# Turning the score matrices by DMA at both ends of a window-attention backward kernel, with its first loads and weight products in another order

## The chip, the cores and the metric

The kernel runs on one core of a Trainium2 chip. The metric is the device time of one execution in microseconds (us); of several runs the median is taken. A core has five engines that are used here: TensorE (PE; its weight loads are shown as a row of their own, PEld), VectorE (DVE), ScalarE (ACT), GpSimd (POOL) and SyncE (SP, which only issues DMAs). Each works through its own instructions in order and waits for the others by semaphores. ACT and POOL issue DMAs from their queues too.

## What is computed

The forward pass is windowed attention without heads: an image of 256 x 256 positions and 384 channels is cut into 8 x 8 windows of 64 tokens, 1024 of them. The kernel returns the output and the gradients of x, wqkv and wo for a given gradient of the output, all in bfloat16.

```python
qkv = xw @ wqkv                       # xw: (1024, 64, 384)
q, k, v = qkv[..., :C], qkv[..., C:2 * C], qkv[..., 2 * C:]
p = softmax(einsum('bqc,bkc->bqk', q, k) * C ** -0.5, axis=-1)
o = einsum('bqk,bkc->bqc', p, v) @ wo
# reference: (o, *vjp of o with respect to x, wqkv, wo, applied to grad_out)
```

## The kernel before

**Weights are multiplied with each other first.** With A = scale * Wq Wk^T and B = Wv Wo (both 384 x 384), the scores of a window are x A x^T, its output is P (x B), and the backward pass needs only A, B and their transposes AT and BT. So the kernel begins with turning weight blocks on PE (`turn_blocks`, L94) and multiplying them (`weight_product`, L101): BT and A first; B and AT come in `weight_rest` (L112), which runs inside the first full step.

**Tiles.** 128 partitions hold two windows. Four such pairs make a quad (8 windows, 512 tokens); there are 128 quads, numbered i. For each quad the kernel holds xq and dq (tokens of x and of the gradient on partitions), xT and dT (the same turned, channels on partitions), yz (the projections of dT by BT and of xT by A, channels on partitions), zy (yz in another order, written by VectorE in `gather`), tok (zy turned back to tokens by DMA), ps (P and dS, bfloat16) and PS (P and dS turned). Loads are in `load` (L123: x by SP, the gradient by POOL; in the loop, half of x by ACT in `load_rest`, L131). xT and dT are made by transposing DMAs from SP's queue (`load_turn`, L135), except for the first quads, whose numbers are below X_ON_PE = 1 and G_ON_PE = 4: these are turned on PE (`turn_on_pe`, L143).

**The loop is pipelined by hand.** `step(c, b, a, ahead)` (L346) writes out the order for three quads at once, c = i - 1, b = i, a = i + 1, and starts the loads of quad i + 3. In the order of PE:

- scores of b (`scores`, L180: the tile sd, both x A x^T and the gradient of P), after which VectorE and ScalarE run the softmax and its backward in six pieces (`soft`, L192);
- eight products x B and x AT of b (`uv`, L227: uq and vq), each emptied by ScalarE (L235);
- three products dT BT of a, emptied by ScalarE into yz (L165), then three products xT A (L167); between them in the program stand the end of the softmax and `turn` (L237);
- one row of a finished group's weight gradient (`gf_rows`, L308, tile pg), if there is one;
- the attention of c in four parts (`attend`, L254): pw, pu, po and pd, emptied as Wq (ACT), Uq (DVE), o (ACT) and d (both), with halves of a weight-gradient row (`gf_halves`, L316, tile ph) between them.

`turn` on VectorE turns P and dS in 32 x 32 blocks: one instruction over the whole tile (L240), four for the crossed blocks (L244). PSUM has a ring of eight banks for all products, so a product waits until the bank that it reuses has been emptied.

**Groups.** Every GQ = 3 quads make a group, whose weight-gradient rows (six, from Uq and Wq) fill the later steps; up to and including the step that scores quad 3 there is nothing to fill with. At the end, rows that are left over run after the loop (L474), then the last group's six rows (`gf_final`, L330) and the products that make the weight gradients (`weight_gradients`, L399), stored by SP and ACT.

**The order at the start** (L437 to L452): weights by SP and ACT, nine warm-up products, loads of quads 0, 1 and 2, the turn and product for BT, the turns of quad 0 (dq, then xq), the turns and product for A, the clearing of GF_acc on VectorE. The loop begins at i = -1, a step with only an `a`, which projects quad 0; after the steps i = -1, 0 and 1 the dq of quads 1, 2 and 3 are turned on PE (L462).

Of the kernel before, what the change touches and what calls it, by code (L numbers as in the profile page):

```python
# [9 lines left out]
ALU = mybir.AluOpType  # L10
# [13 lines left out]
def kernel(  # L24
# [47 lines left out]
    def columns(k):  # L72
        return slice(k * C, (k + 1) * C)

    def fetch_weights():
        nc.sync.dma_start(out=w_sb[:, :, columns(2)], in_=w_in[:, :, columns(2)])
        nc.scalar.dma_start(out=wo_sb[:], in_=wo.rearrange("(m p) n -> p m n", p=P))
        for k in (0, 1):
            nc.scalar.dma_start(out=w_sb[:, :, columns(k)], in_=w_in[:, :, columns(k)])

    def warm_up(n):
        zero = B_sb[:].rearrange("p m c -> p (m c)")[:, 0:4 * P]
# [27 lines left out]
                copy_out(mr, dst[:, mr, :], pc[:])  # L110

    def weight_rest():  # L112
        weight_product(B_sb, wT[2], wo_sb, None)
        weight_product(AT_sb, wT[1], wT[0], scale)

    def windows(ap, st, first, count=2):
        row, col = st["at"]
        return ap[0, row + WIN * first:row + WIN * (first + count), col:col + WIN, :]

    LO, HI = slice(0, WT), slice(WT, P)  # L120
    OTHER = {0: HI, WT: LO}

    def load(st, on_act=0):  # L123
        st["xq"] = xq = grp.tile([P, QUAD, C], BF16, tag="xq", name="xq", bufs=2 * GQ + 4)
        st["dq"] = dq = qp.tile([P, QUAD, C], BF16, tag="dq", name="dq", bufs=6)
        for t in range(QUAD):
            if t < QUAD - on_act:
                nc.sync.dma_start(out=xq[:, t, :], in_=windows(x, st, 2 * t))
            nc.gpsimd.dma_start(out=dq[:, t, :], in_=windows(grad_out, st, 2 * t))  # L129

    def load_rest(st, on_act):  # L131
        for t in range(QUAD - on_act, QUAD):
# [56 lines left out]
    def over_k(ap, n=P):  # L189
        return ap.unsqueeze(2).broadcast_to([n, QUAD, WT])  # L190

    def soft(st, step):  # L192
        sd = st["sd"]
        if step == 0:
            st["mx"] = mx = sm.tile([P, QUAD], F32, tag="mx", name="mx")
            for w, h in ((0, HI), (1, LO)):
                nc.vector.tensor_reduce(out=mx[h, :], in_=sd[h, :, w, :], axis=AX.X, op=ALU.max)
        elif step == 1:
            mx = st["mx"]
            st["sh"] = sh = sm.tile([P, QUAD, WT], F32, tag="sh", name="sh")  # L200
            for w, h, o in ((0, HI, LO), (1, LO, HI)):
                nc.vector.tensor_tensor(out=sh[o, :, :], in0=sd[h, :, w, :], in1=over_k(mx[h, :], WT),
                                        op=ALU.subtract)
        elif step == 2:
            st["ex"] = ex = sm.tile([P, QUAD, WT], F32, tag="ex", name="ex")
            nc.scalar.activation(out=ex[:], in_=st["sh"][:], func=ACT.Exp)
        elif step == 3:
            ex = st["ex"]
            rs = sm.tile([P, QUAD], F32, tag="rs")
            nc.vector.tensor_reduce(out=rs[:], in_=ex[:], axis=AX.X, op=ALU.add)  # L210
            ri = sm.tile([P, QUAD], F32, tag="ri")
            nc.vector.reciprocal(out=ri[:], in_=rs[:])
            st["ps"] = ps = qp.tile([P, 2, QUAD, WT], BF16, tag="ps", name="ps")
            st["Pb"], st["dS"] = ps[:, 0, :, :], ps[:, 1, :, :]
            nc.vector.tensor_tensor(out=st["Pb"], in0=ex[:], in1=over_k(ri[:]), op=ALU.mult)
        elif step == 4:
            st["pr"] = pr = sm.tile([P, QUAD, WT], F32, tag="pr", name="pr")
            for w, h in ((0, LO), (1, HI)):
                nc.vector.tensor_tensor(out=pr[h, :, :], in0=sd[h, :, w, :], in1=st["Pb"][h, :, :], op=ALU.mult)  # L219
            st["D"] = D = sm.tile([P, QUAD], F32, tag="D", name="D")  # L220
            nc.vector.tensor_reduce(out=D[:], in_=pr[:], axis=AX.X, op=ALU.add)
        else:
            pd = sm.tile([P, QUAD, WT], F32, tag="pd")
            nc.vector.tensor_tensor(out=pd[:], in0=st["Pb"], in1=over_k(st["D"][:]), op=ALU.mult)
            nc.vector.tensor_tensor(out=st["dS"], in0=st["pr"][:], in1=pd[:], op=ALU.subtract)

    def uv(st, t, part):  # L227
# [9 lines left out]
    def turn(st):  # L237
        ps = st["ps"]
        st["PS"] = dst = qp.tile([P, 2, QUAD, WT], BF16, tag="PS", name="PS")
        nc.vector.transpose(out=dst[:].rearrange("p s t k -> p (s t k)"), in_=ps[:].rearrange("p s t k -> p (s t k)"))  # L240
        for first in range(0, P, WT):
            for q in (0, SQ):
                k = SQ - q
                nc.vector.transpose(out=dst[first + k:first + k + SQ, :, :, q:q + SQ].rearrange("p s t k -> p (s t) k"),  # L244
                                    in_=ps[first + q:first + q + SQ, :, :, k:k + SQ].rearrange("p s t k -> p (s t) k"))

    def operand(st, n, t, h):
        if n in ("PT", "ST"):
            return st["PS"][h, int(n == "ST"), t, :]
        if n in ("z", "y"):  # L250
            return st["tok"][h, int(n == "y"), :, t, :]
        return st[n][h, t, :]
# [93 lines left out]
    def step(c, b, a, ahead):  # L346


        def on(st):
            return (lambda f, *r: f(st, *r)) if st is not None else (lambda f, *r: None)  # L350
        C_, B, A = on(c), on(b), on(a)
        B(scores)
        B(soft, 0)
        if b is not None and c is None:
            weight_rest()
        B(uv, 0, 0)
        B(uv, 0, 1)
        B(soft, 1)
        B(uv, 1, 0)
        B(uv, 1, 1)  # L360
        B(soft, 2)
        B(soft, 3)
        B(uv, 2, 0)
        B(uv, 2, 1)
        B(uv, 3, 0)
        B(uv, 3, 1)
        B(soft, 4)
        for mo in range(CK):
            A(project, 0, mo)
        B(soft, 5)  # L370
        B(turn)
        if ahead is not None:
            load(ahead, ON_ACT)
        A(gather, 0)
        for mo in range(CK):
            A(project, 1, mo)
        if ahead is not None:
            load_rest(ahead, ON_ACT)
        if fill:
            gf_rows(*fill.pop(0))  # L380
        slots = attention(c) if c is not None else iter(())
        for t in range(QUAD):
            if t == 2:
                A(gather, 1)
            next(slots, None)
        for rest in slots:
            pass

    G_ON_PE, X_ON_PE = 4, 1
    ON_ACT = 2  # L390
    EV = {"z": "AAA", "y": "AAA", "u": "AAAA", "v": "AAAA", "o": "AAAA", "U": "DDDD", "W": "AAAA", "d": "DADAA"}
    quads = [(row, col) for col in range(0, W, WIN) for row in range(0, H, 2 * WIN * QUAD)]
    sts = [{"at": q, "i": i} for i, q in enumerate(quads)]
    n = len(sts)
    AHEAD = 3
    dw_out = out_2.rearrange("(m p) j -> p m j", p=P)
    dwo_out = out_3.rearrange("(m p) n -> p m n", p=P)
# [1 line left out]
    def weight_gradients(group):  # L399
# [31 lines left out]
        dw = rows("dw")  # L431
        for k in range(CK):
            product_row(k, dw[:, k, :], GFT[1], woT_sb, None)
            (nc.scalar, nc.sync)[k % 2].dma_start(out=dw_out[:, k, columns(2)], in_=dw[:, k, :])

    with tc.manual_schedule(engines=MANUAL):
        fetch_weights()  # L437
        warm_up(9)
        load(sts[0])
        make_identity(nc, ident[:])  # L440
        load(sts[1])
        load(sts[2])
        load_turn(sts[0])
        load_turn(sts[1])
        turn_blocks(wT[2], w_sb, 2 * CK)
        weight_product(BT_sb, wo_sb, wT[2], None)
        turn_on_pe(sts[0], "dq", "dT")
        turn_on_pe(sts[0], "xq", "xT")
        turn_blocks(wT[0], w_sb, 0)
        turn_blocks(wT[1], w_sb, CK)  # L450
        weight_product(A_sb, wT[0], wT[1], scale)
        nc.vector.memset(GF_acc[:], 0.0)  # L452
        held = []
        last = None
        get = lambda i: sts[i] if 0 <= i < n else None
        for i in range(-1, n + 1):
            if 0 <= i < n - 2:
                load_turn(sts[i + 2])
            if 0 <= i < n:
                to_tokens(sts[i])  # L460
            step(get(i - 1), get(i), get(i + 1), get(i + AHEAD) if i >= 0 else None)
            if 0 < i + 2 < G_ON_PE:  # L462
                turn_on_pe(sts[i + 2], "dq", "dT")
            if i == 1:
                turn_blocks(woT_sb, wo_sb)
            if i > 0:
                held.append(sts[i - 1])
                sts[i - 1] = None
            if held and i == n:
                last = gf_final(held)  # L470
            elif len(held) == GQ:
                fill.extend((held, f, ma) for f in range(2) for ma in range(CK))
                held = []
        while fill:  # L474
            gf_rows(*fill.pop(0))
        weight_gradients(last)


# [28 lines left out]
```

## Time and profile before

| | us |
|---|---|
| median of 3 runs | 1917.22 |
| lowest and highest | 1910.97, 1922.25 |
| the profiled execution | 1913.78 |
| its span, first to last instruction | 1912.0 |
| PE busy | 1897.3 (99%) |
| VectorE busy | 1676.1 (88%) |
| ScalarE busy | 1530.4 (80%) |
| POOL busy | 860.0 (45%) |
| mean granted clock of PE | 0.997 |

Times in the profile count from the start of the span. Busy time of PE counts a product from its start to its modelled end, so overlapping products fill it; a group like "PE L151 MATMUL pj<-xT,A_sb" is named by engine, line, operation, output and input. In brackets behind an instruction stands how long its engine idled before it and who ended that. SPq, ACTq and POOLq are the DMA-issuing parts of these engines; the time from a DMA's issue to its landing is listed apart. Marks in the profiled execution: the first scores at 18.25, those of quad 1 at 30.45, of quad 2 at 46.72, of quad 3 at 59.87 and of quad 4 at 74.69; the last quad's scores at 1868.72; the last rows of the last group from 1893.5; the last copy out of PSUM begins at 1908.38.

### The profile page before, as it was taken

The numbers are of one execution on the slowest core, as the hardware profiler recorded it, in microseconds if no ns is written. First come the engines' busy times: TensorE is split into PE (matmuls) and PEld (weight loads), VectorE is DVE, ScalarE is ACT, GpSimd is POOL, SyncE is SP. The second block draws the span as 40 slices with busy tenths as digits, with TensorE's granted clock in tenths as the row PEclk, the third lists the DMA queues.
The fourth block names the chain that finished last, engine by engine and source line by source line (L and its number), as shares of the span: only waits on it lengthen the run. The fifth ranks groups of instructions, "written<-read, shape, count | busy, mean of one in ns | idle before, by whom it ended". The sixth has DMA issues, their size and how long they took to land.

```text
span 1912.0 us, 57287 instructions
## 1 busy us (share of the span) xinstructions
PE 1897.3 (99%) x22359; PEld 1131.5 (59%) x22359; DVE 1676.1 (88%) x3625; ACT 1530.4 (80%) x3357; POOL 860.0 (45%) x1574
## 2 busy tenths in 40 slices
PE   8999999999999999999999999999999999999998
PEld 5556655655665565556556655655665565556555
DVE  6888888888888888888888888888888888888887
ACT  7878887888788888878887887888788788878884
POOL 3444544444444444444444444444444444445432
PEclk9999999999999999999999999999999999999999
DMA  8999999999999999999999999999999999999993
GB/s 183 200 223 215 221 211 214 232 210 222 200 232 211 225 204 229 217 223 216 224 210 212 225 226 219 206 220 221 223 214 216 223 224 204 210 231 222 206 197 93
DMA packets 943376, 406.91 MB, mean 213 GB/s; under 512 B 825344, under 2 KB 918528, under 8 KB 943104
## 3 DMA queue, kind: packets, MB, share of 16 engines
q1 hardware_dynamic: 830352, 226.46, 77.1%
q0 software_dynamic: 75264, 151.11, 32.6%
q10 hardware_dynamic: 37488, 25.67, 6.0%
q8 instruction: 175, 2.87, 0.7%
q14 instruction: 97, 0.79, 0.1%
HBM read 101.84 MB, written 101.84 MB: 107 GB/s over the span
## 4 chain that ended last, share of the span: by engine, by line
PE 95%; DVE 2%; DMA 1%; ACT 1%; issue 0%; ACTq 0%; SPq 0%
PE pj L151 50%; PE pg L151 13%; PE ph L324 13%; PE sd L151 5%; PE pw L269 5%; PE po L269 4%; PE pu L269 4%; DMA dT<-dq 1%; PE pd L269 1%; DMA xq<-in_x_dram 0%; DVE PS L244 0%; ACTq L133 0%; PE pe L403 0%; DVE pr L219 0%; DVE Uq L283 0%
## 5 line engine op out<-in xcount | busy, mean ns | idle before, releaser
L289 POOL DMA_DIRECT2D out_dram<-o x512 | 274.4, 536 | 795.4 <-ACT o L273 783.6
L280 ACT CAST Wq<-pw 128x384 bf16<-128x384 f32 x512 | 246.6, 482 | 280.7 <-PE pw L269 264.9
L151 PEld LDWEIGHTS <-xT 128*128 128x128 bf16 x3072 | 292.3, 98 | 182.9 <-issue 1.0
L129 POOL DMA_DIRECT2D dq<-in_grad_out_dram x512 | 270.6, 534 | 194.5 <-PE pj L151 86.8
L151 PE MATMUL pj<-B_sb,xT 128*128 128x384 bf16 x1536 | 334.0, 327 | 0.0
L151 PE MATMUL pj<-AT_sb,xT 128*128 128x384 bf16 x1536 | 333.8, 326 | 0.0
L283 DVE CAST Uq<-pu 128x384 bf16<-128x384 f32 x512 | 283.1, 553 | 16.9 <-PE pu L269 4.9
L291 POOL DMA_DIRECT2D out_dram<-d x480 | 277.8, 579 | 16.3 <-ACT uq L235 6.6
L151 PE MATMUL pj<-dT,BT_sb 128*128 128x512 bf16 x1152 | 269.5, 379 | 0.0
L151 PE MATMUL pj<-xT,A_sb 128*128 128x512 bf16 x1152 | 269.5, 379 | 0.0
L269 PE MATMUL pd<-tok,ps 64*64 64x384 bf16 x2048 | 256.4, 327 | 0.7 <-ACT Wq L280 0.6
L165 ACT CAST yz<-pj 128x512 bf16<-128x512 f32 x384 | 224.8, 586 | 37.2 <-PE pj L151 28.6
L273 ACT CAST o<-po 128x384 bf16<-128x384 f32 x512 | 249.3, 487 | 3.8 <-PE po L269 3.6
L235 ACT CAST vq<-pj 128x384 bf16<-128x384 f32 x512 | 247.1, 483 | 3.7 <-PE pj L151 0.5
L235 ACT CAST uq<-pj 128x384 bf16<-128x384 f32 x512 | 244.4, 477 | 3.6 <-PE pj L151 1.8
L167 ACT CAST yz<-pj 128x512 bf16<-128x512 f32 x384 | 225.1, 586 | 23.5
L244 DVE STREAM_TRANSPOSE PS<-ps 32x256 bf16<-32x256 bf16 x512 | 223.2, 436 | 9.7
L151 PEld LDWEIGHTS <-xq 128*128 128x128 bf16 x1572 | 153.6, 98 | 115.0 <-issue 0.6
L324 PEld LDWEIGHTS <-xq 64*64 64x64 bf16 x6000 | 177.5, 107 | 67.0
L324 PE MATMUL ph<-Wq,xq 64*64 64x384 bf16 x3984 | 204.4, 322 | 0.0
L151 PEld LDWEIGHTS <-A_sb 128*128 128x128 bf16 x1152 | 112.7, 98 | 135.9
L151 PEld LDWEIGHTS <-BT_sb 128*128 128x128 bf16 x1152 | 112.7, 98 | 122.3
(85 smaller groups left out, 3066.1 us busy)
## 6 DMA issues: line engine op xcount, KB each, us to landing
dq<-in_grad_out_dram POOLq DMA_DIRECT2D x512, 96.0 KB, 5.8
out_dram<-o POOLq DMA_DIRECT2D x512, 96.0 KB, 5.1
out_dram<-d POOLq DMA_DIRECT2D x480, 96.0 KB, 5.4
xq<-in_x_dram SPq DMA_DIRECT2D x262, 96.0 KB, 4.9
xq<-in_x_dram ACTq DMA_DIRECT2D x250, 96.0 KB, 6.0
out_dram<-d POOLq DMA_DIRECT2D x64, 48.0 KB, 5.4
tok<-zy SPq DMA_TRANSPOSE x128, 10.3
xT<-xq SPq DMA_TRANSPOSE x127, 7.6
```

The costliest lines, as they stand in the source:

```text
L129: nc.gpsimd.dma_start(out=dq[:, t, :], in_=windows(grad_out, st, 2 * t))
L151: nc.tensor.matmul(out, lhsT=lhsT, rhs=rhs, start=start, stop=stop)
L165: ENG[EV["z"][mo]](out=yz[:, mo, :, 0:4:3, :], in_=pj[:])
L167: ENG[EV["y"][mo]](out=yz[:, mo, :, 1:3, :], in_=pj[:])
L235: cp(out=dst[:, t, :], in_=pj[:])
L269: nc.tensor.matmul(dst[o, :], lhsT=operand(st, lhs, t, h), rhs=operand(st, rhs, t, h), **flags)
L273: copies[EV[name][i]](out=sb[rows, :], in_=src[rows, :])
L280: copies[EV["W"][t]](out=st["Wq"][:, t, :], in_=pw[:])
L283: copies[EV["U"][t]](out=st["Uq"][:, t, :], in_=pu[:])
L289: nc.gpsimd.dma_start(out=windows(out_0, st, 2 * t), in_=o)
L291: nc.gpsimd.dma_start(out=windows(out_1, st, 2 * t - 1), in_=d if t else above[:])
L324: nc.tensor.matmul(dst[o, :], lhsT=st["xq"][h, t, ma * P + o.start:ma * P + o.stop], rhs=st["UW"[f] + "q"][h, t, :], start=(i == 0), stop= ...
```

## The change

**P and dS by DMA.** Quads 0, 1, 2 and 127 are marked `crossed`. For them ScalarE copies P (two copies of 64 partitions) and VectorE writes dS a second time (two subtractions of 64 partitions) into a tile cr with one buffer, in which the halves of the partitions are arranged so that one transposing DMA from SP's queue writes PS. VectorE's five turning instructions are left out for these quads. The DMA stands in SP's queue where `turn` stands in the step, ahead of the loads of quad i + 3.

**The start.** The third column block of wqkv and wo are fetched first, split over SP and ACT; then the gradient of quad 0 (SP and ACT); then the other two blocks of wqkv; x of quad 0, half by SP and half by POOL. POOL is made to wait by small copies into a tile `spare`: for the last gradient tile of quad 0 before its half of x, and for the second tile of x before it issues the gradients of quads 1 and 2. GF_acc is cleared on POOL. Seven warm-up products take the place of nine, and ACT's first copy is moved ahead.

**Order on PE.** The step i = -1 is written out and split: quad 0's dT is projected as soon as it is there, then the weights for A are turned and multiplied, then xT is turned and projected, then dq of quad 1 is turned. G_ON_PE is 2 for 4: dT of quads 2 and 3 comes by DMA. B and AT are no longer products but turns of BT and A (nine 128 x 128 turns each for nine 128 x 384 products each), and stand ahead of the first scores.

**The tail.** In the two last steps, which have no `a`, two weight-gradient rows run ahead of the attention for one; none is left for after the loop. The last three stores alternate beginning with SP for ACT.

In `load`, the four DMAs of the gradient are written ahead of those of x; they are on different engines.

```diff
@@ fetch_weights
-        nc.sync.dma_start(out=w_sb[:, :, columns(2)], in_=w_in[:, :, columns(2)])
-        nc.scalar.dma_start(out=wo_sb[:], in_=wo.rearrange("(m p) n -> p m n", p=P))
-        for k in (0, 1):
-            nc.scalar.dma_start(out=w_sb[:, :, columns(k)], in_=w_in[:, :, columns(k)])
+        wo_in = wo.rearrange("(m p) n -> p m n", p=P)
+        nc.sync.dma_start(out=w_sb[:, 0:2, columns(2)], in_=w_in[:, 0:2, columns(2)])
+        nc.scalar.dma_start(out=w_sb[:, 2, columns(2)], in_=w_in[:, 2, columns(2)])
+        nc.scalar.dma_start(out=wo_sb[:, 0:2, :], in_=wo_in[:, 0:2, :])
+        nc.sync.dma_start(out=wo_sb[:, 2, :], in_=wo_in[:, 2, :])
+
+    def fetch_rest():
+        nc.sync.dma_start(out=w_sb[:, :, columns(0)], in_=w_in[:, :, columns(0)])
+        nc.scalar.dma_start(out=w_sb[:, :, columns(1)], in_=w_in[:, :, columns(1)])
@@ weight_rest
-        weight_product(B_sb, wT[2], wo_sb, None)
-        weight_product(AT_sb, wT[1], wT[0], scale)
+        turn_blocks(B_sb, BT_sb)
+        turn_blocks(AT_sb, A_sb)
@@ new
+    def load_first(st):
+        st["xq"] = xq = grp.tile([P, QUAD, C], BF16, tag="xq", name="xq", bufs=2 * GQ + 4)
+        st["dq"] = dq = qp.tile([P, QUAD, C], BF16, tag="dq", name="dq", bufs=6)
+        for t in range(QUAD):
+            (nc.sync, nc.scalar)[t % 2].dma_start(out=dq[:, t, :], in_=windows(grad_out, st, 2 * t))
+        fetch_rest()
+        for t in range(2):
+            nc.sync.dma_start(out=xq[:, t, :], in_=windows(x, st, 2 * t))
+        nc.gpsimd.tensor_copy(out=spare[:, 0:1], in_=dq[:, QUAD - 1, 0:1])
+        for t in range(2, QUAD):
+            nc.gpsimd.dma_start(out=xq[:, t, :], in_=windows(x, st, 2 * t))
+        nc.gpsimd.tensor_copy(out=spare[:, 1:2], in_=xq[:, 1, 0:1])
@@ soft, last piece
+            if st["crossed"]:
+                st["cr"] = cr = qp.tile([P, QUAD, 2, WT], BF16, tag="cr", name="cr", bufs=1)
+                for w, h, o in ((0, LO, HI), (1, HI, LO)):
+                    nc.scalar.copy(out=cr[h, :, w, :], in_=st["Pb"][h, :, :])
+                    nc.vector.tensor_tensor(out=cr[o, :, w, :], in0=st["pr"][h, :, :], in1=pd[h, :, :], op=ALU.subtract)
@@ turn
+        if st["crossed"]:
+            whole = dst[:].rearrange("p s t k -> p (s t k)").rearrange("p (t s k) -> p t s k", t=QUAD, s=2)
+            st["PS"] = whole.rearrange("p t s k -> p s t k")
+            nc.sync.dma_start_transpose(out=whole.rearrange("p t s k -> p t (s k)"),
+                                        in_=st["cr"][:].rearrange("p t w k -> p (t w k)"))
+            return
@@ step
         C_, B, A = on(c), on(b), on(a)
+        if b is not None and c is None:
+            weight_rest()
         B(scores)
         B(soft, 0)
-        if b is not None and c is None:
-            weight_rest()
...
-        if fill:
-            gf_rows(*fill.pop(0))
+        for rows in range(1 if a is not None else 2):
+            if fill:
+                gf_rows(*fill.pop(0))
@@ constants
-    G_ON_PE, X_ON_PE = 4, 1
+    G_ON_PE, X_ON_PE = 2, 1
...
+    sts = [{"at": q, "i": i, "crossed": i < GQ or i == n - 1} for i, q in enumerate(quads)]
@@ weight_gradients
-            (nc.scalar, nc.sync)[k % 2].dma_start(out=dw_out[:, k, columns(2)], in_=dw[:, k, :])
+            (nc.sync, nc.scalar)[k % 2].dma_start(out=dw_out[:, k, columns(2)], in_=dw[:, k, :])
@@ schedule
+        spare = sm.tile([P, 3], BF16, name="spare", bufs=1)
         fetch_weights()
-        warm_up(9)
-        load(sts[0])
+        warm_up(7)
+        nc.scalar.copy(out=spare[:, 2:3], in_=B_sb[:, 0, 0:1])
         make_identity(nc, ident[:])
+        nc.gpsimd.memset(GF_acc[:], 0.0)
+        load_first(sts[0])
...
         turn_on_pe(sts[0], "dq", "dT")
-        turn_on_pe(sts[0], "xq", "xT")
+        for mo in range(CK):
+            project(sts[0], 0, mo)
         turn_blocks(wT[0], w_sb, 0)
         turn_blocks(wT[1], w_sb, CK)
         weight_product(A_sb, wT[0], wT[1], scale)
-        nc.vector.memset(GF_acc[:], 0.0)
+        turn_on_pe(sts[0], "xq", "xT")
+        gather(sts[0], 0)
+        for mo in range(CK):
+            project(sts[0], 1, mo)
+        gather(sts[0], 1)
+        turn_on_pe(sts[1], "dq", "dT")
...
-        for i in range(-1, n + 1):
+        for i in range(n + 1):
...
-            step(get(i - 1), get(i), get(i + 1), get(i + AHEAD) if i >= 0 else None)
-            if 0 < i + 2 < G_ON_PE:
-                turn_on_pe(sts[i + 2], "dq", "dT")
+            step(get(i - 1), get(i), get(i + 1), get(i + AHEAD))
```

More of the change, by code (lines that the diff above doesn't have):

```diff
@@ L126, in load @@
         for t in range(QUAD):
-            if t < QUAD - on_act:
-                nc.sync.dma_start(out=xq[:, t, :], in_=windows(x, st, 2 * t))
             nc.gpsimd.dma_start(out=dq[:, t, :], in_=windows(grad_out, st, 2 * t))
+        for t in range(QUAD - on_act):
+            nc.sync.dma_start(out=xq[:, t, :], in_=windows(x, st, 2 * t))
     def load_rest(st, on_act):
@@ L248, in operand @@
         if n in ("PT", "ST"):
-            return st["PS"][h, int(n == "ST"), t, :]
+            return st["PS"][h, int((n == "ST") == (h == LO or not st["crossed"])), t, :]
         if n in ("z", "y"):
@@ L392 @@
     quads = [(row, col) for col in range(0, W, WIN) for row in range(0, H, 2 * WIN * QUAD)]
-    sts = [{"at": q, "i": i} for i, q in enumerate(quads)]
-    n = len(sts)
+    n = len(quads)
+    sts = [{"at": q, "i": i, "crossed": i < GQ or i == n - 1} for i, q in enumerate(quads)]
     AHEAD = 3
```

## The prediction

> **What bounds the kernel now.** I read the page first, then the chain of waits, then the start and the end of the timeline. The chain that ended last is TensorE almost everywhere:
>
> ```profile
> span 1912.0 us, 57287 instructions
> ...
> PE 95%; DVE 2%; DMA 1%; ACT 1%; issue 0%; ACTq 0%; SPq 0%
> ```
>
> One step of the loop (scores of one quad to scores of the next) lasts 14.56 us when all is running (74.69 to 89.25), filled by PE without a gap. The change leaves that step alone, so no gain can come from the 123 steps between 74.69 and 1868.7. What is left is 74.7 us ahead of them and 43.3 us behind. I call T0 to T4 the starts of the scores (sd) of quads 0 to 4; before: 18.25, 30.45, 46.72, 59.87 and 74.69. In these steps the filler products (pg, ph) don't exist yet, PE has some 10.7 us of work in each, and takes 13 to 16. The chain of waits says on whom it waits (start, duration, what):
>
> ```profile
> 53.62 0.72 DVE PS L240
> ...
> 56.18 0.56 DVE zy L173
> ...
> 56.77 0.56 DVE Uq L283
> ...
> 59.87 1.40 PE sd L151 x24
> ```
>
> VectorE turns P and dS (53.62 to 56.15, 2.5 us), and only then empties the banks of the attention that PE already runs. The second cost is the clock. In the table by stage, columns are length, busy time of PE, PEld, DVE, ACT, POOL, the granted clock, DMA share and GB/s:
>
> ```profile
> 39.28:42.69 3.41, 1.39 (x24) 0.64 (x25) 3.24 (x8) 2.00 (x5) 0.55 (x1) 0.99 1.08 225
> 42.69:46.10 3.41, 3.40 (x37) 2.46 (x37) 2.94 (x7) 3.15 (x9) 3.15 (x6) 0.51 1.03 201
> 56.35:59.76 3.41, 1.82 (x28) 0.86 (x27) 3.31 (x7) 3.21 (x8) 2.09 (x4) 0.99 1.19 132
> 59.76:63.18 3.42, 3.42 (x35) 2.33 (x32) 2.31 (x6) 1.80 (x5) 2.65 (x6) 0.51 1.05 278
> 69.99:73.41 3.42, 1.96 (x37) 0.93 (x36) 3.27 (x8) 2.59 (x8) 0.83 (x2) 1.00 1.19 201
> 1875.60:1879.06 3.46, 1.55 (x36) 0.86 (x29) 3.32 (x8) 1.35 (x3) 0.53 (x1) 0.99 0.10 28
> 1879.06:1882.47 3.41, 3.41 (x44) 2.26 (x47) 1.97 (x5) 1.48 (x4) 1.59 (x3) 0.51 0.21 57
> ```
>
> After 3.41 us with PE busy 1.39, 1.82 or 1.55 us, the next 3.41 us run at half clock; after 1.96 they don't. Price: T2 to T3 took 13.15, the step T3 to T4, alike but begun at half clock, 14.82, so 1.6 a time.
>
> ScalarE is nearly as full as VectorE there:
>
> ```profile
> 47.94 0.48 ACT L235 CAST uq<-pj 128x384 bf16<-128x384 f32 x1 [0.70 <-PE pj L151]
> ...
> 52.06 1.83 ACT L165 CAST yz<-pj 128x512 bf16<-128x512 f32 x3 [0.22 <-PE pj L151]
> 53.95 1.88 ACT L167 CAST yz<-pj 128x512 bf16<-128x512 f32 x3
> 55.25 1.20 ACTq L133 DMA_DIRECT2D xq<-in_x_dram  x2
> 56.48 0.48 ACT L280 CAST Wq<-pw 128x384 bf16<-128x384 f32 x1 [0.66 <-PE pu L269]
> ```
>
> **The change part by part.**
>
> *Start, up to T0.* Nothing before T0 leaves PE's queue but two warm-up products; 18 transposes come in (B and AT turned from BT and A). I follow PE's queue with the rows' durations. Seven warm-ups end at 4.2 (1.20 + 7 x 0.43). The first weights took 4.2 from issue to landing beside much else; over two queues and alone I put them at 4.35 (no earlier than 4.2, no later than before's 4.95). Turns 0.55; ScalarE's copy of wT, behind four DMA issues of 0.5 of which two wait for landings, ends at 5.7; the other eight products 1.35, to 7.1; dq's turns 0.67, to 7.8 (dq now goes ahead of the rest, so before's waits of 0.22, 0.89 and 0.17 go); last copy of dT at 8.4; projection 1.95, to 10.4; 18 turns of the other weights 1.0; ScalarE's copies, behind three yz, at 11.9; A's products 1.35, to 13.25; x's turns to 13.9, the last copy of xT at 14.6; projection to 16.6; dq of quad 1 to 17.3; the 18 new turns 1.0 (18 such take 1.17 with their ends): 18.3, as before. I keep T0 = 18.25; bounds 0.7 earlier (weights at 4.2, copies not waited for) and 2 later (the first dq or x land 7.1 after issue, the longest early row, for the median 5.6, and the weights no sooner than before). The clearing of GF_acc on POOL: 1.98 on DVE's row, 4.3 by POOL's memset of ident (0.24 for 128 columns, 18 times); either ends before the landing that POOL waits for next, about 7. That wait and the next one hold back the dq of quads 1 and 2; issued by about 10.3, they land by 16 (5.6 median), and PE wants them at 16.6: no cost, but no cover either.
>
> *T0 to T1.* The 18 products that made B and AT (19.29 to 22.05, 2.76) are gone, so uq begins at about 19.75. ScalarE then does 8 evictions and the exp (3.9, to 23.65), yz for three banks (PE delivers at 23.8; 1.83), the two new copies cr, and yz again (1.88). The scores of quad 1 need the last yz. The copies' shape is not in the trace: exp of 128x256 comes every 0.33, a 64-partition eviction every 0.38, a plain one lasts 0.49; a pair costs 0.66 to 0.98, I take 0.7. T1 = 23.8 + 1.83 + 0.7 + 1.88 = 28.2.
>
> *T1 to T3.* VectorE loses 2.5 of turning and the 0.62 of dT copies, gains 0.88 (two subtractions, as L202). By its rows it would now have Uq's turn free at T+8.4, when PE begins the attention: **it no longer bounds. ScalarE does.** In the built program the next scores wait for the bank of the fourth Wq eviction. Count of one step: first uq at T+1.22, 3.9, gap 0.2, yz 1.85, cr 0.7, yz 1.9, DMA issue 0.65, and four Wq among o and d, 0.375 apart, done after 3.1. T2 = 28.2 + 13.5 = 41.7, plus 0.2 for woT's turns: 41.9. Then o, two d and woT precede the next uq (43.2), no gap: T3 = 43.2 + 3.9 + 1.85 + 0.7 + 1.9 + 0.65 + 3.1 = 55.3. The step is no shorter than before's 13.15: here the new copies cost what the turns cost.
>
> *T3 to T4.* Quad 3 is turned as before: exp ends 58.7, VectorE's chain to the end of PS 5.95 (50.20 to 56.15), zy and Uq 1.2, two more Uq 2.15, last product 0.42: T4 = 68.4.
>
> *Clock.* PE still idles in these attentions, 1.4, 1.9 and 1.4 us by the count above, against 1.5 in one window that brings half clock. I charge one window of 1.6: **T4 = 70.0, gain 4.7** (none: 6.3; three: 1.5).
>
> [...]
>
> *The turns by DMA.* PS joins SP's queue between tok and the xq of the quad three ahead; SP waits there for cr. Those xq loads move some 3 us, but xT waits for ScalarE's half of xq anyway. dT of quads 2 and 3 are added too, where DMA before moved 4 GB/s (26.0 to 30.4 us). Landings: dT and xT 4.1 to 11.4 (7.4 median), tok up to 15.6. PS, a third of xT's size, may be below 4.1; I take 7.4. Issued at about 26.3, 38, 51.5, needed 11, 11 (by the next cr, one buffer) and 12.7 later: hidden.
>
> *Tail.* Now PE waits where the last quad's turning on VectorE holds up Uq:
>
> ```profile
> 1878.97 0.46 PE L269 MATMUL pu<-xq,PS 64*64 64x384 bf16 x1 [1.91 <-DVE GF_acc L306]
> ```
>
> and pays with the half clock to 1882.47. From the first pg (1873.45) the work is four pg of 1.95 and two attentions with ph of 3.75: 15.3, ending 1888.75; it ended 1893.5, 4.75 lost. After, two pg stand ahead of each attention: VectorE ends dS at 1876.65 (0.88 later), adds, and has Uq at 1877.98, 0.7 after the attention's start, against 0.6 in a full step. New: the first final row needs the last Uq, 1.3 after the attention's end, when 7 of its 8 products (1.14) are done: 0.2, and 0.2 for a weight load. **Gain 4.3** (3.0 to 4.75). PS of the last quad has 8.4 us. The queues of the last dw: DVE's last copy (1908.30) waits for PE's last product as before: 0.
>
> Sum: 4.7 + 4.3 = 9.0. The profiled execution took 1913.78 (span 1912.0), so 1904.8 by it; it lies 3.4 under the median of the runs, 1917.22, so **1908.2** against that.
>
> **Rivals.** (a) *ScalarE and the clock eat the lead*: half clock after all three attentions; for: idle 1.4 is close to 1.5; against: idle comes in more, shorter pieces. Gain 1.5 + 4.3: 1911.4. (b) *All goes well*: T0 0.7 earlier, no half clock: 11.3, 1905.9. (c) *The first loads don't come in order of use in time*: T0 2 later: 1910.2; for: POOL's two waits in a row. (d) *Slower: the DMA turn replaces the VectorE turn as the wait*. If PS lands like tok's longest row, 15.6, PE or ScalarE waits 4.6, 4.6, 2.9 and in the tail 7.2: 19.3, so 10.3 slower, 1927.5. It decides from landings of about 13 (2 + 2 + 0.3 + 4.6 = 8.9, the whole gain). For: DMA share over 1 from 40 us on, and one tok there took 14.0; against: the queue is idle when the first is issued, and in the tail 0.1 busy.
>
> **How the numbers follow.** Forecast 0.47, (a) 0.24, (b) 0.15, (c) 0.09, (d) 0.05. The range takes in (a), (b) and (c) with the runs' own spread of 5 us either way: 1900 to 1917. Half a per cent, 9.6 us, is about what a measurement of this kernel tells from none. The forecast's own spread (7 to 11) lies across it, with two fifths beyond: faster 0.15 + 0.19 = 0.34 and a little of (a) by chance, 0.36; slower 0.05; same 0.59.
>
> **What would show it.** Right: scores of quads 1 to 4 near 28, 42, 55 and 70; ScalarE without gaps and VectorE with gaps from 29 to 55; no half clock behind 1870, and gf_final from 1884.5 with all shifted by the lead. Wrong: steps of 11 us there (cr cheaper, banks free earlier); PE or ScalarE waiting for DMA PS; T0 off by over 1; steps other than 14.56 between.

## The result and the profile after

| | before | after |
|---|---|---|
| median of 20 runs, us | 1913.66 | 1911.26 |
| lowest and highest | 1910.97, 1923.94 | 1905.35, 1918.85 |
| the profiled execution | 1913.78 | 1905.65 |
| its span | 1912.0 | 1903.9 |
| mean granted clock in it | 0.997 | 1.000 |
| ratio of the runs | | 0.9977 (95%: 0.9966 to 0.9988) |

By the ratio, which rests on more than the two middle runs, the changed kernel is 4.4 us faster (2.3 to 6.5; the medians alone lie 2.4 apart); I had said 9.0. Ratios leave out slow runs, those more than 1.5% above the fastest of their kernel: three of ten in e11 and two of the 35 of before in the last set, none elsewhere. Of the profiled executions the second is 8.1 shorter, so the pair shows almost the whole forecast and the twenty runs half of it. A second set of runs of the same kernel (e5, below) gave 0.9961 (0.9945 to 0.9977), 7.5 us.

The page of the changed kernel answers the first lines of the prediction: the chain still runs through TensorE, with one hundredth of the span less for VectorE and one more for TensorE.

```profile
span 1903.9 us, 57253 instructions
...
PE 96%; DMA 1%; ACT 1%; DVE 1%; ACTq 0%; issue 0%; SPq 0%
```

The marks, first product of the scores each (T0 to T4) and the last quad's: 18.87, 27.6 (all but two of its 24 products wait until 28.55), 42.2, 55.4, 68.7; 1864.6. So T4 is 5.9 earlier than before's 74.6, the stretch to the last scores 1.7 longer (1795.8 for 1794.1), and the tail 4.0 shorter (39.3 for 43.3). All marks from here on are the starts of the first product of the scores; the prediction read its marks of before from pieces of the chain of waits, and its 46.72 for quad 2 is 46.55 by this count.

In the lead ScalarE is on the chain, as the chain of waits shows for the step from T1 to T2 (start, duration, what):

```profile
28.55 0.81 PE sd L169 x22
...
35.73 0.40 ACT cr L246
...
36.15 0.40 ACT cr L246
...
36.57 1.07 ACT yz L185 x2
...
39.01 0.49 ACT Wq L309
```

Between the two copies of P and the first Wq eviction ScalarE has no gap; the attention that PE has begun at 37.1 waits for that eviction. VectorE now has gaps (1.12 us before 32.31, 0.64 before 37.66), where in the lines shown of before it turned for 2.5 us.

In the tail the chain goes straight through the attention (it was held there by VectorE in before) and shows the one new wait that the prediction named, the first row of gf_final for the last Uq:

```profile
1877.41 4.01 PE pg L169 x24
...
1884.67 0.55 DVE d L302
...
1885.21 0.48 DVE GF_acc L335
...
1885.71 0.56 DVE GF_acc L335
...
1886.27 0.47 DVE Uq L312
...
1886.79 4.22 PE pg L169 x25
```

### The profile page after: what moved, and what is told of

Same layout as the page of the kernel before. It is cut to its first block, busy times and chain, and to the rows that moved or that the text cites. A ratio compares the mean times of both kernels' runs of the same rounds, so it can differ in the third digit from the quotient of the medians.

```text
span 1903.9 us, 57253 instructions
## 1 busy us (share of the span) xinstructions
PE 1890.4 (99%) x22333; PEld 1126.9 (59%) x22333; DVE 1665.9 (87%) x3610; ACT 1528.7 (80%) x3360; POOL 859.1 (45%) x1575
## 4 chain that ended last, share of the span: by engine, by line
PE 96%; DMA 1%; ACT 1%; DVE 1%; ACTq 0%; issue 0%; SPq 0%
PE pj L169 51%; PE pg L169 13%; PE ph L353 13%; PE sd L169 5%; PE pw L298 5%; PE po L298 4%; PE pu L298 4%; DMA dT<-dq 1%; PE pd L298 1%; PE pe L433 0%; ACTq L151 0%; ACT yz L185 0%; DMA wo_sb<-in_wo_dram 0%; ACT Wq L309 0%; PE pt L103 0%
## 5 line engine op out<-in xcount | busy, mean ns | idle before, releaser
L183 ACT CAST yz<-pj 128x512 bf16<-128x512 f32 x384 | 224.9, 586 | 38.2 <-PE pj L169 29.6
L273 DVE STREAM_TRANSPOSE PS<-ps 32x256 bf16<-32x256 bf16 x496 | 216.2, 436 | 9.5
```

Of the source, the lines that this page charges most:

```text
L183: ENG[EV["z"][mo]](out=yz[:, mo, :, 0:4:3, :], in_=pj[:])
```

## The experiments

My theory after the result: the lead gains 2.8 us between T0 and T1 by the turned weights; from there ScalarE's copies cost what VectorE's turn cost; the tail gains by both of its parts; and half-clock windows, which come or not by the phase of a fixed grid, make the profiled pair look better than the runs. The rival was that the DMA turn is what shortens the lead. There are twelve experiments in three sets, with 6 to 12 runs each (e1 has 6; e5 is the changed kernel once more); each set has runs of the kernel before on the same chip, and "before" has medians of 1914.37, 1914.85 and 1914.32 there.

To make marks comparable I take out the half clock: 1.6 us for each 3.41 us window that ended ahead of the mark, half of what had run of one that hadn't ended. "Tail" is from the last quad's scores to the end, without half clock. "Clock" is the mean granted clock over the runs; one window in a run is 0.0009.

| | T1 | T2 | T3 | T4 | T4 without half clock | tail | clock | ratio to before (95%) |
|---|---|---|---|---|---|---|---|---|
| before | 30.5 | 46.6 | 59.8 | 74.6 | 71.4 | 41.7 | 0.9978 to 0.9980 | 1 |
| after | 27.6 | 42.2 | 55.4 | 68.7 | 68.7 | 39.3 | 0.9985 | 0.9977 (0.9966 to 0.9988) |
| e1 no DMA turn | 27.8 | 42.4 | 55.6 | 69.7 | 69.0 | 40.8 | 0.9998 | 0.9960 (0.9945 to 0.9975) |
| e2 tail as before | 28.0 | 43.6 | 57.0 | 70.3 | 68.7 | 41.7 | 0.9980 | 0.9986 (0.9972 to 0.9999) |
| e3 two rows, last quad on VectorE | 27.6 | 42.5 | 55.6 | 68.9 | 68.9 | 40.5 | 0.9985 | 0.9979 (0.9961 to 0.9997) |
| e4 cr on GpSimd | 27.3 | 41.3 | 56.3 | 75.7 | | 39.3 | 0.9968 | 0.9989 (0.9973 to 1.0006) |
| e5 after again | 27.6 | 42.8 | 56.4 | 69.9 | 67.9 | 39.3 | 0.9993 | 0.9961 (0.9945 to 0.9977) |
| e6 DMA turn alone | 30.6 | 45.7 | 58.3 | 71.7 | 71.7 | 40.5 | 0.9988 | 0.9984 (0.9973 to 0.9996) |
| e7 B, AT by products | 29.6 | 44.5 | 57.0 | 71.3 | 70.7 | 39.2 | 0.9986 | 0.9980 (0.9966 to 0.9994) |
| e8 e1, two Uq on ScalarE | 27.4 | 42.4 | 55.5 | 68.7 | 68.7 | 40.7 | 0.9991 | 0.9972 (0.9957 to 0.9987) |
| e9 DMA turn for the last quad alone | 27.7 | 42.3 | 55.5 | 68.8 | 68.8 | 39.3 | 0.9996 | 0.9959 (0.9941 to 0.9978) |
| e10 before, PE filled | 30.1 | 46.8 | 61.9 | 77.0 | 77.0 | 42.1 | 0.9988 | 1.0031 (1.0011 to 1.0052) |
| e11 all quads by DMA | 28.0 | 42.8 | 55.8 | 68.3 | 68.3 | 39.4 | 0.9978 | 1.0017 (0.9986 to 1.0047) |
| e12 e9, PE filled | 27.5 | 43.9 | 59.0 | 74.1 | 74.1 | 39.3 | 0.9997 | 0.9985 (0.9968 to 1.0002) |

Raw marks repeat within a few tenths, marks from which half clock was taken out within 0.8 (T4 of after, e2, e3 and e5: 68.7, 68.7, 68.9, 67.9); the ratios are known to 0.2% or so (4 us). What is worth 1 to 3 us is read from the marks. For e4 no T4 without half clock is given: PE waits for others in parts of its two double windows, so 1.6 a window is not their price.

### e1: no quad turned by DMA

```diff
-"crossed": i < GQ or i == n - 1}
+"crossed": False}
```

> The changed kernel, but no quad is turned by DMA: P and dS of all quads are turned on VectorE, and the copies cr are gone. My theory (ScalarE bounds the steps after T1, the cr pair of 0.82 us is what it has too much): T1 0.8 earlier (27.7), steps of 12.5 to 12.7 by ScalarE's rows less 0.8 and by VectorE's step of before (13.15) less the 0.62 of dT copies, so T2 near 40.4, T3 near 53, T4 near 66.2 for 68.8: the lead is 2.4 shorter than the changed kernel's. The tail, where VectorE turns for 2.5 instead of writing cr for 0.85, is about 1.0 longer. In all 1.4 faster than the changed kernel. Rival (VectorE bounds these steps, and the DMA turn is what shortens them): T2, T3 and T4 each come 1.65 later a step, T4 near 72, and the kernel is about 4.8 slower than the changed kernel.

T2 and T3 are those of the changed kernel within 0.3, and so is T4 without half clock: neither theory. (Later expectations give e1's T4 as 68.1; that took off 1.6 for a window of which only 1.44 us had run by T4. It is 69.0.) The rival is out: without the DMA turn nothing in the lead is later by more than 0.3 (half clock taken out). My own count was out too: ScalarE without its copies is not 0.8 earlier. The chain of waits in e1, same step:

```profile
29.41 7.80 PE pj L169 x42
...
37.23 0.57 ACT yz L185
...
37.84 1.29 ACTq L151
...
39.18 0.48 ACT Wq L309
```

PE's 42 products run without a gap, as in the changed kernel. ScalarE finishes yz 0.3 earlier (37.80 for 38.13), but then its two issues of x take until 39.13, where they ended at 38.96 with the copies. VectorE is without a gap from 32.2 to 42.9. So two engines and the issues behind them reach the first Wq at the same time with either way of turning. The tail is 1.5 longer.

### e2 and e3: the tail in parts

```diff
-        for rows in range(1 if a is not None else 2):
+        for rows in range(1):
...
-"crossed": i < GQ or i == n - 1}
+"crossed": i < GQ}
```

e2 has both edits, e3 only the second.

> The changed kernel with the tail of before: one weight-gradient row ahead of each attention, the last quad turned on VectorE. Theory: last scores to the end 43.3 us with a half-clock window (as in the profile of before) or 41.7 without, against 39.3, so 2.4 to 4.0 slower than the changed kernel, and the lead as in the changed kernel. Rival (the tail gained only because the profile of before had a half-clock window there and that of after had none): 39.3 to 40.9, at most 1.6 slower.

> The changed kernel, with the last quad turned on VectorE; the two rows stay ahead of the attention. Theory (two rows ahead give most of the tail's gain, the turn by DMA the rest): last scores to the end 40.3, 1.0 longer than the changed kernel's 39.3, since VectorE comes to Uq 1.65 later than 0.7 us into the attention. Rival (the DMA turn makes the gain): 41.7 or more.

The old tail takes 41.7 without half clock, the two rows alone 40.5 to 40.8 (e3, e8, e1), the DMA turn alone 40.5 (e6), both 39.3: 0.9 to 1.5 each by the pairs of runs, and they add to 2.4. The profile of before had a half-clock window there too, which makes the 4.0. Both expectations hold for the tail, and the rival of e2 (all of it the clock) is out: e2's tail has no half-clock window and takes 41.7.

### e4: the copies of P on GpSimd

```diff
-                    nc.scalar.copy(out=cr[h, :, w, :], in_=st["Pb"][h, :, :])
+                    nc.gpsimd.tensor_copy(out=cr[h, :, w, :], in_=st["Pb"][h, :, :])
```

> The changed kernel with the two copies of P into cr on GpSimd in place of ScalarE. Theory (ScalarE bounds the lead): T1 0.8 earlier, each step to quad 3 0.8 shorter, so T4 about 66.3 for 68.8, 2.4 faster than the changed kernel, if GpSimd does a copy within about 1 us and the DMA turn stays hidden. Rival (ScalarE has slack, and VectorE or a landing sets the steps): T2 to T4 within 0.5 of the changed kernel's, no gain; or slower, if GpSimd, which issues the stores and loads, comes to cr late and the DMA turn becomes the wait.

T2 is 1.0 earlier, as a ScalarE bound wants it (1.6 by my count). Then the DMA turn becomes the wait, which was my rival (d). SP's queue in e4 (timeline):

```profile
53.26 6.76 SPq L195 DMA_TRANSPOSE tok<-zy  x1
60.19 1.55 SPq L266 DMA_TRANSPOSE PS<-cr  x1
```

The step T2 to T3 (15.0) waits for PS itself. In the chain of waits the landing of one PS lets VectorE write the next cr (the tile has one buffer), and dS, zy, Uq and PE follow behind that:

```profile
44.77 6.09 DMA PS<-cr
...
50.98 0.13 DVE cr L247
...
52.98 0.56 DVE Uq L312
...
54.18 0.48 PE pw L298
```

The step T3 to T4 (19.4) waits for another DMA. SP's queue is late by now, so dT is issued at 63.33 (56.30 in the changed kernel's same step); ScalarE's issue of x waits for its landing, and Wq and PE wait behind that:

```profile
63.33 7.51 DMA dT<-dq
...
70.86 0.55 ACTq L151
...
72.81 0.49 ACT Wq L309
...
73.34 0.48 PE pd L298
```

In the step of the SP lines cr was complete at 52.2; PS is issued at 60.2, behind the issue of tok (6.8 us here, 4.2 in the changed kernel's same step). The three of the lead land 6.1 to 7.5 after issue for 3.6 to 4.4. GpSimd can write cr again only at 35.44 and 51.01, just behind the landing of the last PS (35.28 and 50.86), and issues the gradient loads behind that; why the DMAs got slower with it stays open.

### e5: the changed kernel again

> The changed kernel once more, on the same chip as the next three. Theory (the profiled pair overstated the gain: half-clock windows come on a fixed 3.41 us grid whose phase differs from run to run, and one comes after a window in which products, weighted by the part of the array that they use, fill less than a third; the profile of before had 3 of these windows where its average over all phases is 1.8, that of after 0 where its average is 0.5): the median of the runs lies 4 to 7 below that of before, the mean clock of the runs is below 1.000, and the marks T1 to T4 come within 0.7 of 27.6, 42.2, 55.4, 68.7 plus 1.6 for every such window that the profile shows. Rival (the steps between are longer in the changed kernel): the stretch from T4 to the last scores is 2 or more above 1794.1 in nearly every profile.

The median lies 8.7 below that of before (ratio: 7.5), more than the 4 to 7 expected. This profile has two half-clock windows (from 41.8 and 69.1) where the first had none. The stretch from T4 is 1795.2, 1.1 above before's, but one profile doesn't settle the rival: of the ten profiles of the changed kernel and its variants, leaving out e11, six lie 2 or more above it. The runs tell more. With half clock taken out by the mean clock (1.6 us for each 0.0009 below 1), e5's mean lies 4.8 below that of before in its set; lead and tail give 2.8 + 2.4 = 5.2 by the marks. Over the seven experiments e1 to e3, e5 and e7 to e9 the runs fall 0.4 short of what each one's own T4 and tail give, on average (1.1 short to 1.0 over). So by the runs longer steps between cost the changed start about half a microsecond, and the rival is out as the main cause. The two intervals have 4.4 to 6.5 us in common.

### e6: the DMA turn alone

The kernel before with the change's last piece of `soft`, its `turn` and its `operand`, which picks the half of PS that belongs to the rows in the new layout, and

```diff
-    sts = [{"at": q, "i": i} for i, q in enumerate(quads)]
-    n = len(sts)
+    n = len(quads)
+    sts = [{"at": q, "i": i, "crossed": i < GQ or i == n - 1} for i, q in enumerate(quads)]
```

> The kernel before with nothing but the DMA turn of quads 0, 1, 2 and 127: start, weight products and the order of the tail as before. Theory (the copies cr on ScalarE cost in the lead what the turn on VectorE cost): T4 within 1.0 of before's 71.4 (74.6 less two half-clock windows of 1.6, plus 1.6 for every one that this profile has before T4); last scores to the end 40.3 to 41.0, 0.7 to 1.4 below before's 41.7 without a window, as VectorE comes 1.65 earlier to Uq; in all 0.5 to 3 faster than before. Rival (VectorE's turn bounds these steps, so the DMA turn is what shortens them): each of the steps T1 to T2 and T2 to T3 1.65 shorter, T4 near 68, in all 5 faster or more.

T4 71.7 for 71.4 without half clock, tail 40.5: theory right, rival out. In the lead the DMA turn brings nothing up to T4 here either. The runs are 3.1 faster (0.8 to 5.2): 1.2 is the tail, and the mean clock (0.9988 for before's 0.9978 in this set) says 1.1 half-clock windows fewer, 1.8 us.

### e7: B and AT by products

```diff
-        turn_blocks(B_sb, BT_sb)
-        turn_blocks(AT_sb, A_sb)
+        weight_product(B_sb, wT[2], wo_sb, None)
+        weight_product(AT_sb, wT[1], wT[0], scale)
```

In `step`, `weight_rest` stands behind the first scores again.

> The changed kernel with B and AT made by products behind the first scores, as before, instead of turns ahead of them. Theory (the 2.76 us of products between the first scores and the first uq are what the lead gained): T0 1.0 earlier (17.9), T1 2.0 to 2.8 later than the changed kernel's 27.6, and all marks behind it as much, so 2 to 3 slower than the changed kernel. Rival (the products run while PE waits for the softmax anyway): T1 within 0.5, no difference.

T0 17.9, T1 29.6, T4 70.7 without half clock: 1.0 earlier, then 2.0 later than the changed kernel. That is the largest part of the 2.8 that the lead gains without half clock, and the runs point the same way (0.9980 for e5's 0.9961, 3.6 us, with intervals that overlap). The remaining 0.8 belongs to the rest of the start: the order of the first loads, quad 0's projection split in two, and dT of quads 2 and 3 by DMA. These were not tried apart.

### e8: two of four Uq on ScalarE

```diff
-copies[EV["U"][t]](out=st["Uq"][:, t, :], in_=pu[:])
+copies[("DADA" if st["i"] < GQ else EV["U"])[t]](out=st["Uq"][:, t, :], in_=pu[:])
```

> As e1 (the changed kernel, all quads turned on VectorE), and two of the four Uq evictions of quads 0, 1 and 2 on ScalarE instead of VectorE. Theory (without the DMA turn VectorE, gapless from 28 to 42 us in e1's profile, bounds the steps, and ScalarE has 1.4 us free ahead of its first Wq): each of the three steps T1 to T4 about 0.7 shorter than e1's 14.6, 13.2 and 12.5 (without half-clock window), T4 near 66 for e1's 68.1, 2 faster than e1. Rival (ScalarE bounds as soon as it has two more evictions): T4 within 0.6 of 68.1.

T4 68.7 for e1's 69.0: the rival. Neither engine alone holds the lead; work taken from one is missing on the other.

### e9: the DMA turn for the last quad alone

```diff
-"crossed": i < GQ or i == n - 1}
+"crossed": i == n - 1}
```

> The changed kernel with the DMA turn kept for the last quad alone; quads 0, 1 and 2 are turned on VectorE. Theory (in the lead the DMA turn gains nothing, in the tail it gains 1.2): T1 to T4 as in e1 (27.8, 42.4, 55.6, 68.1, plus 1.6 for every half-clock window before T4), last scores to the end 39.3 as in the changed kernel for 40.8 in e1; the median within 2 of the changed kernel's on this chip (e5: 0.9961 of before). Rival (the DMA turn of the first quads gives 3 or more): ratio to before 0.998 or above, T4 71 without a half-clock window.

As expected: T2 to T4 as with the DMA turn, tail 39.3, and 8.0 below before in the medians. It is as fast as the changed kernel, with three turns less. Whether it is faster can't be told (0.9959 with 0.9941 to 0.9978, against 0.9961 and 0.9977).

### e10 and e12: filling PE

```diff
+    def warm_bank(st, out):
+        for k in range(2 if st["i"] < GQ else 0):
+            nc.tensor.matmul(out[:], lhsT=BT_sb[:, 0, 0:P], rhs=A_sb[:, 0, :], start=True, stop=True)
...
         pu = bank("pu")
+        warm_bank(st, pu)
...
         po = bank("po")
+        warm_bank(st, po)
```

> The kernel before, with four products more of 128 x 128 x 384 in each part of the attention of quads 0, 1 and 2, whose result is overwritten: 48 products, 7.7 us of work for PE where it waits anyway. Theory (half clock comes after a window that fills less than a third of the array, 0.188 to 0.281 at the least in these attentions; the products add 0.64 us to each part, so at the least 0.19 to a window): no half-clock window before T4, for 1.17 expected without the filler (2 of the 3 in the profile of before); T4 between 71.4 and 73 for 74.6; the mean clock of the runs rises by about 0.001 from 0.9978. In time 0 to 1.9 faster, so no more than hardly measurable. Rival (the clock goes by idle time alone, not by how much of the array is in use, or the filler's products delay the evictions): half-clock windows before T4 as before, T4 74.6 or later, up to 7.7 slower.

> As e9, with the filler of e10 in the attention of quads 0, 1 and 2. Theory: no half-clock window before T4 and a mean clock of the runs above e9's; T4 68 to 69 in every case; the best version here, by 0 to 1.5 below e9, which this number of runs can't tell from nothing, so by its profile. Rival (the filler delays the evictions): T4 0.7 or more above e9's time without half clock.

In e10 the clock did as said: no half-clock window before T4, and the mean clock of the runs is 0.9988 for before's 0.9979 in this set, 0.9 windows fewer where 1.1 were due. e12 tells nothing of the clock (0.9997 for e9's 0.9996, and e9's profile has no window before T4 either). In both PE became the bound (in e10 it is busy 13.77 of the 14 us from 36 on): each step takes 1.8 to 2.3 more, so T4 comes 5.6 (e10) and 5.4 (e12) later than in the kernels they were built from, without half clock. So T4 went the rival's way in both, and the runs are 0.3% slower than those of before (e10) and than e9's (e12, with intervals that overlap). A smaller filler than 0.64 us a part was not tried.

### e11: all quads by DMA

```diff
-"crossed": i < GQ or i == n - 1}
+"crossed": True}
```

> The changed kernel with the DMA turn for all 128 quads. Theory (the DMA queues are near their limit in the full steps, share 1.20 and late landings that stop ScalarE and PE now and then; a turn more in each step makes the landings later): steps longer than 14.56, 1 to 4 per cent slower. Rival (PE bounds the full steps, and a landing of 3 to 7.5 us has 11 us of cover): steps of 14.56 as before, within 0.3 per cent of the changed kernel.

Half right. The median step stays 14.57, the rival's number, but 15 steps take 15.2 to 18.8. By the ratios the kernel is 0.4 to 0.6% slower than the changed one (8 to 11 us), less than the 1 per cent that I gave as the least and more than the rival's 0.3. The median of all its ten runs is 1923.14; they go from 1902.53 to 1945.79. VectorE is relieved (busy 75% for 87%) and no other engine gets faster by it. Who waits, from the rows on the tile cr in e11 (us in all, times):

```profile
who waited for it (us, times):
  DVE cr L247: 84.0, 37
  ACT cr L246: 60.9, 32
...
DMA to landing us min/median/max: 2.4/5.5/8.8
```

The next cr waits for the last PS to land: the tile has one buffer, and PS is issued late behind tok (tok's issue from 549.69 to 557.72, PS at 557.88).

## Why the prediction was right, and where not

*Time.* 1911.26 lies in the range, and "same" (within half a per cent) was called the likeliest. The gain of 9.0 was too high for the runs (4.4 and 7.5).

*Start.* T0 18.25, measured 18.87. Off by 0.6: ScalarE's copy of wT behind its DMA issues ended at 6.0 for the 5.7 of the count, and another 0.3 gathers in small pieces behind it (the last copy of dT ends at 8.8 for 8.4, that of xT at 15.1 for 14.6). PE's waits for these copies (0.67, 0.57 and 0.66) were in the count. GF_acc on POOL took 2.01, and POOL's waits cost nothing.

*T1 to T4.* Predicted without half clock 28.2, 41.9, 55.3, 68.4; measured 28.55 (last part), 42.2, 55.4, 68.7. The copies cr were 0.82 a pair for 0.7. "Here the new copies cost what the turns cost" holds: e1, e6 and e9. "It no longer bounds. ScalarE does" holds for the chain of the changed kernel (e4: T2 1.0 earlier), but it is too simple: taken away, the copies bring nothing (e1), since the issues of x and VectorE stand just behind.

*Clock: the step that was mis-sized.* I charged the changed kernel one window and left before its three. Both were taken from one execution, and by busy time, which is the wrong measure. The rows below are 3.41 us windows and their successors; columns as in the prediction's table. First e1, then e2:

```profile
37.56:40.97 3.41, 1.95 (x36) 0.86 (x29) 3.27 (x8) 2.04 (x6) 0.64 (x1) 1.00 1.16 245
40.97:44.38 3.41, 3.38 (x53) 2.30 (x49) 2.96 (x9) 3.40 (x10) 3.41 (x8) 1.00 1.05 184
```

```profile
38.00:41.41 3.41, 2.38 (x33) 0.94 (x24) 2.45 (x5) 2.16 (x7) 0.47 (x1) 1.00 1.28 203
41.41:44.83 3.42, 3.39 (x44) 2.51 (x43) 1.99 (x5) 2.99 (x9) 3.42 (x8) 0.50 1.05 257
```

Behind the first window, in which PE is busy 1.95 us, the clock stays full; behind the other, in which it is busy 2.38, half clock follows. What separates the two, by my count, is how much of the array is in use. I counted each product as its columns at 2.4 a nanosecond (my rounding of 2.36: 24 products of 384 columns take 3.90 us in before from 1893.44 on) times the part that it fills of 128 x 128, the largest form in the traces; the 64 x 64 products of the attention fill a quarter each, and four run beside each other (in before four begin within 0.01 us at 100.074, the next four 0.16 later). By that count the first window is 0.344 full and the second 0.303.

I did this for all 14 profiles, for the windows at full clock behind 15 us and ahead of the end of the work. Half clock follows each of the 16 that are filled up to 0.341; it follows none of the others, of which 12 are filled 0.344 to 0.40. The rule is fitted to these profiles, and 0.34 belongs to this way of counting: with each product counted back from its modelled end, the two groups overlap (up to 0.368 and from 0.358). The one test ahead of its result is e10.

The windows lie on a grid of 3.413 us (before's second and third begin 5 and 538 periods behind its first), and the grid's phase differs from run to run (half clock begins at 42.65 in before, at 41.41 in e2, at 41.76 in e5). So I slid such a window over each profile and counted the phases that bring half clock, with a third as the limit: 1.8 windows for before (0.71 in the tail, and 0.71, 0.19 and 0.19 in the three attentions of the lead), 0.5 for after, 0.7 to 0.8 for e5. The profile of before had 3, that of after 0: by this count 1.7 windows, 2.7 us, of the 8.1 are the phases' luck. On the average the change gains 71.4 - 68.6 = 2.8 in the lead (mean of after, e2, e3 and e5), 41.7 - 39.3 = 2.4 in the tail and 1.0 to 1.3 windows, 1.6 to 2.1: about 7, if the steps between are as long in both.

*The base.* I added 3.4 because the median of three runs was 1917.22. The median of twenty is 1913.66, just the profiled execution; 1904.8 was the forecast by the execution, which measured 1905.65, and 1908.2 came nearer to the median of the runs by chance. That 1904.8 fits the execution is luck too: its lead gained 5.9 for 4.7, its tail 4.0 for 4.3, and its steps between lost 1.7 that I had at nothing.

*The rest between 4.4 and 7.* The steps between T4 and the last scores are 14.57 in the median in both kernels, but in most profiles one or more is longer: from T4 to the last scores it is 1793 to 1803, 1808 in e9 and 1820 in e11. In e9 (chain of waits) a late landing of dT holds ScalarE's issue of x, and that holds Wq and PE:

```profile
808.03 9.33 DMA dT<-dq
...
817.38 0.55 ACTq L151
...
817.97 1.40 ACTq L151
...
819.41 0.49 ACT Wq L309
```

PE idled 4.25 us there, and half clock followed (16 products ph took 1.79 for the 0.82 of the part ahead). In the trace this issue of x waits for the semaphore on which dT's landing is told, and takes it for its own DMA: SP's and ScalarE's DMAs share eight (107, 109, 111 to 115 and 117 in before). So one of ScalarE's two issues of x waits for dT in nearly every step (122 or 123 a run) of every kernel here but e11's, and in 14 to 28 steps a run it comes just as dT lands (22 in before, 20 in after).

PE's long gaps (0.6 us or more) behind 90 us and ahead of the last scores sum to 0 in before's profile, 2.4 in after's, 0 in e5's, 4.7 in e7's. They come in kernels with and without the DMA turn (e1: 2.9). For the first set of after the mean clock says 1.7 windows a run, where 0.5 to 0.8 are due to lead and tail; without half clock its mean lies 2.9 to 3.8 below those of before in the other sets, for the 5.2 of lead and tail. Both point to such gaps in some of its runs, but only one of them was profiled. Why that set gained less than e5 or e9 stays open.

*The turns by DMA.* PS landed 3.6 to 4.4 after issue in the lead and 2.4 in the tail, for the 7.4 taken; below 4.1 was held possible. It is hidden, as said. What I had not counted is how long tok's issue keeps SP: cr was ready at 50.25 and PS issued at 53.60 (changed kernel, third turn; 51.5 by my count). Rival (d) had the right mechanism and place, the next cr; it needs e4's or e11's conditions.

*Tail.* 4.3 predicted, 4.0 measured between the profiles; 2.4 of it without the clock, so the half clock that I took from one execution is 1.6 of this term too. The row of gf_final that waits for the last Uq begins at 1885.37 and gets it at 1886.74; its seven other products are through by 1886.5, so the new wait is 0.3, for 0.4 allowed.

## What to carry to other kernels

Where two engines each fill a stage, moving work from one to the other can change the chain and not the time (T4 without half clock 69.0, 68.7 and 68.8 in e1, e8 and e9, 68.7 in after). Before a small gain is read off two profiles, take out what differs by phase and chance: here 2.7 of 8.1 us was the clock's grid, by the count above. A transposing DMA with one source buffer was hidden where it landed before that buffer was written again (2.4 to 4.4 us after issue in the changed kernel); issued late behind a longer one, or landing later (6.1 to 7.5 in e4's lead, up to 8.8 in e11), it made the next writer wait. A second buffer was not tried.

## What the runs showed of the hardware that I had not expected

- In these 14 profiles half clock followed each 3.413 us window whose products filled up to 0.341 of the array by the count above, and none that was filled 0.344 or more, though PE may count as busy for most of it (e5: 2.50 us in 38.34 to 41.76, 0.326 full).
- The issue of tok's transposing DMA kept SP for 3.7 to 8.5 us (median 5.8, after), that of the PS turn for 1.2 to 1.4; behind tok in SP's queue PS was issued at 53.60 for cr ready at 50.25 (after), and at 60.2 for 52.2 (e4).
- GpSimd's copy of 64 x 256 in bfloat16 took 0.39 to 0.65 (e4), ScalarE's 0.40 (after).
- In e9 a DMA's issue waited to 817.38 for the landing (817.36) of one that it has no data in common with, but shares a semaphore: ScalarE's x behind dT.
